# One 4.5 MB weight load made as eight interleaved loads of sixteen rows each

## The chip, the cores and the metric

The kernel runs on one core of one Trainium2 chip. The metric is the device time of one execution in microseconds (us); the lower the better. Times are medians of several runs.

## The reference

Two independent problems, A and B, have the same shapes, and their results are put side by side. Each is one decoding step of attention with a sliding window over a cache:

```python
W = min(4096, max(256, Sk // 4))                       # 4096 of 16384 cached positions
q = (x @ wq).reshape(B, 1, Hq, Dh).transpose(0,2,1,3)  # x 2x1x576, wq 576x4096
k = repeat(k_cache[:, :, Sk - W:, :], 2, axis=1)       # 2x16x16384x128 -> 32 heads
v = repeat(v_cache[:, :, Sk - W:, :], 2, axis=1)
p = softmax(einsum("bhqd,bhkd->bhqk", q, k) * Dh ** -0.5)
o = einsum("bhqk,bhkd->bhqd", p, v)
out = o.transpose(0,2,1,3).reshape(B, 1, Hq * Dh) @ wo # wo 4096x576
# result: concatenate([A, B], axis=-1)
```

All inputs are bf16. B is 2, Hq 32, Hkv 16, Dh 128. Nearly all bytes are the windows of k_cache and v_cache: 2 problems x 2 batches x 16 heads x 4096 x 128 x 2 bytes, twice, which is 134 MB. The two wq are 4.7 MB each and the two wo as much.

## The kernel before, in words

The program is written as lists of operations, one list for each engine, in an order set by hand (`_Sched`, lines 28 to 58). Each operation names the operations that it depends on; `emit` puts semaphore waits ahead of it. A transfer adds 16 to its semaphore when it has landed, so whoever needs it waits for 16 times the number of transfers (`dma_op`, which counts with `n_dmas`).

**The load queue.** All large loads are issued by SyncE (SP), in program order, onto one queue that the 16 DMA engines serve: first wq of A (`wq0`), then wq of B (`wq1`), both at line 187, then the stream of cache slabs at line 378 (K0, K1, K2, then K and V in turn, 16 of each, 4 MB a slab), with blocks of wo (line 362) between them. ScalarE's queue carries only the small loads of x (line 179) and one store.

**The ring.** A tile `ring` of four slots of 128 partitions x 32 KB takes the slabs. Before the slabs it holds the two wq, each spread over 128 partitions with 36,864 bytes (9 blocks of 2048 bf16) in each: partition p gets the p-th of 128 equal parts of wq's bytes. So wq0 and wq1 lie over the first three slots. Slab K0 goes to the fourth slot and waits for nothing. K1 goes to the first slot and waits until the matmuls of wq0 are done (`first_deps`); K2 waits for those of wq0 and wq1. From then on SP issues a slab when the last reader of its slot is done.

**From wq to q.** DVE spreads x out (`xs`, line 222) and transposes it (`xT`, line 229). TensorE then computes q of problem A from wq0 with 36 matmuls (`q0`, lines 279 and 264), and of problem B from wq1 (`q1`), waiting for `wq_dma[P]`, that is for the semaphore of that load. ScalarE takes q out of PSUM, TensorE transposes and spreads it, and GpSimd makes masked copies of it (`zq`).

**Each K slab** is transposed by DVE in two halves (line 433) and multiplied by q on TensorE (lines 459 and 264). Two slabs (one group of four heads, both batches) give the scores of one softmax: DVE takes the maximum (467), ScalarE the exponentials (497), DVE transposes them (506). **Each V slab** is multiplied by these (536), scaled and reduced on DVE (559, 566). At intervals the heads' results are multiplied by wo (618, 639), and the two outputs are stored.

The change touches the loop at lines 184 to 188, which issues `wq0` and `wq1`:

```python
for P in range(NPROB):
    def f_wq(e, P=P):
        src = probs[P][3].rearrange("a b -> (a b)").rearrange("(p f) -> p f", p=128)
        return e.dma_start(ringf[:, P * QW:(P + 1) * QW], src).then_inc(wq_sem[P], 16)
    wq_dma[P] = dma_op("sp", wq_sem[P], 1, f_wq, [], "wq%d" % P)
```

Its readers are `f_q` (the matmuls of q), which waits for `wq_dma[P]`, and, through the order of SP's queue, every later load.

Of the kernel before, what the change touches and what calls it, by code (L numbers as in the profile page):

```python
# [62 lines left out]
def build_kernel(nc, probs, out):  # L63
# [25 lines left out]
    QW = NU * UW  # L89
# [3 lines left out]
    with es:  # L93
# [50 lines left out]
        ringf = ring[:].rearrange("p r f -> p (r f)")  # L144
# [16 lines left out]
        wq_sem = [sem("wq%d" % P) for P in range(NPROB)]  # L161
# [7 lines left out]
        def dma_op(eng, sem_h, n_dmas, fn, deps, tag):  # L169
            op = S.add(eng, fn, deps, tag)  # L170
            dma_count[sem_h] = dma_count.get(sem_h, 0) + 16 * n_dmas
            op.dma = (sem_h, dma_count[sem_h])
            return op
# [9 lines left out]
        wq_dma = {}  # L183
        for P in range(NPROB):
            def f_wq(e, P=P):
                src = probs[P][3].rearrange("a b -> (a b)").rearrange("(p f) -> p f", p=128)
                return e.dma_start(ringf[:, P * QW:(P + 1) * QW], src).then_inc(wq_sem[P], 16)
            wq_dma[P] = dma_op("sp", wq_sem[P], 1, f_wq, [], "wq%d" % P)

        pool = lambda fn, deps, tag: S.add("pool", fn, deps, tag)  # L190
        dve = lambda fn, deps, tag: S.add("dve", fn, deps, tag)
# [600 lines left out]
def bass_concat_heads__sliding_block_cached__sliding_block_cached__decode_kernel(  # L792
    nc, A_x, A_k_cache, A_v_cache, A_wq, A_wo, B_x, B_k_cache, B_v_cache, B_wq, B_wo, out,
):
    build_kernel(nc, [(A_x, A_k_cache, A_v_cache, A_wq, A_wo), (B_x, B_k_cache, B_v_cache, B_wq, B_wo)], out)
# [28 lines left out]
```

## Time and profile before

| what | value | where from |
|---|---|---|
| median of 3 runs | 363.08 us (362.99 to 363.29) | times |
| span of the profiled execution, first to last instruction | 361.8 us | page |
| median of the runs less that span | 1.3 us | worked out |
| bytes moved by DMA | 153.26 MB, 424 GB/s over the span | page, part 2 |
| share of the 16 DMA engines' time used by SP's queue | 98.7% | page, part 3 |
| TensorE, VectorE, ScalarE busy | 66%, 60%, 13% of the span | page, part 1 |
| granted TensorE clock, mean | 0.849 | view of the cores |
| wq0 from issue to landing | 13.3 us | page, part 6 |
| wq1 from issue to landing | 23.8 us | page, part 6 |

The profile gives no time of the profiled execution but its span; the runs' own times include what lies around the span, and 1.3 us is the difference to their median.

How to read the views: the page's part 2 cuts the span into 40 slices and gives, for each, the share of time that the engines and the 16 DMA engines were busy (in tenths) and the GB/s moved. Part 3 adds up the packets of each DMA queue: q1 is SP's queue, q10 ScalarE's. Here one row of a transfer, that is the contiguous bytes for one partition, is one packet, and each DMA engine that took part in a transfer adds a packet of 4 bytes, which increments the semaphore. Part 6 lists the transfers by the line that issued them, with their size and the median time from issue to landing. The timeline lists instructions in order of time; SPq and ACTq are the issues of transfers on SP's and ScalarE's queues. The windows give each engine's busy time, the DMA share and the GB/s in stretches of the span.

### The profile page before, as it was taken

The page shows a single profiled execution, that of the slowest core. Times are in us where ns is not written, and L with a number is a line of the kernel's source. Part 1 is how long each engine was busy: PE and PEld are TensorE (multiplying, and loading weights), DVE is VectorE, ACT ScalarE, POOL GpSimd, SP SyncE. Part 2 cuts the span into 40 slices and gives each one's busy share as a digit, 9 for nine tenths or more (in the row PEclk, how much of TensorE's full clock was granted, in tenths as well). Part 3 has the DMA queues.
Part 4 walks back from the last instruction along what each step waited for, and adds up shares of the span by engine and source line. Part 5 has one row for each costly group of instructions (what it writes and reads, how often), then busy time and mean ns, then how long its engine had stood idle before and what let it go on. Part 6 is the DMA issues. An engine that isn't in the chain of part 4 may idle for free.

```text
span 361.8 us, 2625 instructions
## 1 busy us (share of the span) xinstructions
PE 240.2 (66%) x1292; PEld 57.2 (16%) x927; DVE 218.7 (60%) x150; ACT 46.0 (13%) x78; POOL 24.3 (7%) x84
## 2 busy tenths in 40 slices
PE   0497787666485747662596675567776875668695
PEld 0000111112111201111121121112112121112222
DVE  1901898495929591934909585682927776674622
ACT  1002100040023000500005000500005000500500
POOL 4200101100010001000010000100010001000000
PEclk9999698969988996888788796888688796868969
DMA  8999999999999999999999999999999999999996
GB/s 327 457 435 406 460 408 446 424 431 438 417 453 408 457 404 428 444 431 431 435 420 444 417 449 410 440 431 438 424 442 412 449 417 429 435 435 431 417 412 256
DMA packets 6227, 153.26 MB, mean 424 GB/s; under 512 B 700, under 2 KB 840, under 8 KB 1224
## 3 DMA queue, kind: packets, MB, share of 16 engines
q1 hardware_dynamic: 6196, 153.10, 98.7%
q8 instruction: 8, 0.13, 0.1%
q14 instruction: 3, 0.02, 0.0%
q10 hardware_dynamic: 20, 0.01, 0.0%
HBM read 153.10 MB, written 0.00 MB: 423 GB/s over the span
## 4 chain that ended last, share of the span: by engine, by line
DMA 48%; DVE 26%; PE 16%; issue 8%; ACT 1%; POOL 0%; SPq 0%
DMA ring<-in_B_k_cache_dram 17%; DVE xt L433 16%; DMA ring<-in_A_k_cache_dram 13%; DMA ring<-in_B_v_cache_dram 9%; DMA ring<-in_B_wq_dram 7%; PE st L264 5%; PE st L459 5%; DMA wob<-in_B_wo_dram 3%; PE pj L264 2%; DVE oR L566 2%; DVE mx L467 2%; DVE pT L506 2%; DVE tmp L559 2%; PE ot L536 2%; PE pj L618 1%
## 5 line engine op out<-in xcount | busy, mean ns | idle before, releaser
L459 PE MATMUL st<-xt,zq 128*128 128x512 bf16 x256 | 124.1, 485 | 86.1 <-DVE xt L433 86.1
L433 DVE STREAM_TRANSPOSE xt<-ring 128x4096 f32<-128x4096 f32 x32 | 141.5, 4427 | 28.0 <-DMA ring<-in_A_k_cache_dram 18.8
L264 PE MATMUL st<-xt,zq 128*128 128x512 bf16 x256 | 122.7, 479 | 0.0
L497 ACT ACTIVATE pR<-st,bias 128x512 bf16<-128x512 f32 x32 | 40.0, 1414 | 222.9 <-DVE bias L490 222.9
L459 PEld LDWEIGHTS st<-xt,zq 128*128 128x128 bf16 x256 | 29.4, 115 | 210.1 <-issue 107.7
L536 PE MATMUL ot<-ring,pT 128*32 128x512 bf16 x512 | 32.6, 396 | 3.9 <-DMA ring<-in_B_v_cache_dram 3.9
L490 DVE SCALAR_TENSOR_TENSOR bias<-vmask,tb,offm 128x4 f32<-128x4 f32 x8 | 1.8, 223 | 43.0 <-PE tb L487 43.0
L520 DVE TENSOR_REDUCE ssum<-tb 128x2 f32<-128x8 f32 x8 | 1.3, 162 | 36.0 <-PE tb L517 36.0
L425 POOL TENSOR_TENSOR zq<-qs,bmask 128x64 bf16<-128x64 bf16 x32 | 8.7, 293 | 168.1 <-PE st L264 145.8
L506 DVE STREAM_TRANSPOSE pT<-pR 128x2048 bf16<-128x2048 bf16 x8 | 18.4, 2303 | 0.8 <-ACT pR L497 0.7
L279 PE MATMUL ot<-ring,pT 128*32 128x512 bf16 x18 | 7.6, 421 | 15.0 <-DMA ring<-in_A_wq_dram 14.2
L559 DVE SCALAR_TENSOR_TENSOR tmp<-ot,rsb,dmask 128x512 f32<-128x512 f32 x16 | 11.5, 719 | 7.9 <-PE ot L536 7.9
L566 DVE TENSOR_REDUCE oR<-tmp 128x128 f32<-128x512 f32 x15 | 15.6, 1042 | 0.5
L536 PEld LDWEIGHTS ot<-ring,pT 128*32 128x32 bf16 x512 | 12.4, 99 | 19.6 <-DMA ring<-in_B_v_cache_dram 5.5
L618 PE MATMUL pj<-wob,oM 128*2 128x288 bf16 x48 | 12.7, 299 | 0.0
L264 PE MATMUL pj<-wob,oM 128*2 128x288 bf16 x48 | 12.7, 299 | 0.0
L264 PE MATMUL pj<-ring,pT 128*32 128x512 bf16 x36 | 11.9, 416 | 0.0
L467 DVE TENSOR_REDUCE mx<-st 128x2 f32<-128x1024 f32 x8 | 9.7, 1213 | 0.1
L497 ACT ACTIVATION_READ_ACCUMULATOR pR<-st,bias 128x1 f32 x32 | 8.8, 276 | 0.0
L264 PE MATMUL st<-ring,pT 128*32 128x512 bf16 x18 | 7.3, 407 | 0.0
L222 DVE TENSOR_TENSOR xt<-xt,hmask 4x1152 bf16<-4x1152 bf16 x2 | 2.7, 1349 | 6.7 <-DMA xt<-in_A_x_dram 6.7
L469 POOL TENSOR_TENSOR mv<-mx,v 128x2 f32<-128x2 f32 x8 | 1.6, 195 | 75.8 <-DVE mx L467 75.8
(68 smaller groups left out, 75.6 us busy)
## 6 DMA issues: line engine op xcount, KB each, us to landing
ring<-in_A_k_cache_dram SPq DMA_DIRECT2D x8, 4096.0 KB, 24.3
ring<-in_A_v_cache_dram SPq DMA_DIRECT2D x8, 4096.0 KB, 29.9
ring<-in_B_k_cache_dram SPq DMA_DIRECT2D x8, 4096.0 KB, 27.0
ring<-in_B_v_cache_dram SPq DMA_DIRECT2D x7, 4096.0 KB, 29.8
ring<-in_A_wq_dram SPq DMA_DIRECT2D x1, 4608.0 KB, 13.3
ring<-in_B_wq_dram SPq DMA_DIRECT2D x1, 4608.0 KB, 23.8
wob<-in_A_wo_dram SPq DMA_DIRECT2D x2, 2304.0 KB, 28.3
wob<-in_B_wo_dram SPq DMA_DIRECT2D x1, 2304.0 KB, 27.4
```

The source lines that it names most:

```text
L264: return e.add_instruction(mybir.InstMatmult(name=nc.get_next_instruction_name(), engine=mybir.EngineType.PE, ins=[e.lower_ap(mv_), e.lowe ...
L279: last = e.matmul(QB[c], wt, mv_, start=first, stop=True, skip_group_check=True)
L425: last = e.tensor_tensor(dst, src, msk, ALU.mult)
L433: Xop[(t, jh)] = dve(lambda e: e.transpose(xt[:, jh, :].bitcast(FP32).rearrange("p (kp x kt) -> p x kp kt", kp=2, kt=2), ring[:, r, jh * H ...
L459: last = e.matmul(ob, wt, mv_, start=first, stop=True, skip_group_check=True)
L467: ch[(G, "max")] = dve(lambda e: e.tensor_reduce(mx[:], st[:, :].rearrange("p (x t) -> p t x", t=2), AX.X, ALU.max), [Sop[(2 * G + 1, 1)]] ...
L497: last = e.activation(pR[:].rearrange("p (x k) -> p k x", k=4)[:, kv, :], st[:, :].rearrange("p (x t) -> p t x", t=2)[:, kv % 2, :], ACTF.Exp,
L506: pT_op[G] = dve(lambda e: e.transpose(pT[:, v, :].rearrange("p (w j q) -> p j w q", w=4, q=8), pR[:].rearrange("p (j w q) -> p j w q", w= ...
L536: last = e.matmul(OTB[32 * c:32 * c + 32, :], pT[:, v, base + 32 * c:base + 32 * c + 32], ring[:, r, jj * 128:(jj + 4) * 128], start=rd == ...
L559: evac_op[i] = dve(lambda e: e.scalar_tensor_tensor(tv, o, rsb[:, v, b:b + 1], dm, ALU.mult, ALU.mult), deps, "ev%d" % i)
L566: ch[(G, "red%d" % b)] = dve(lambda e: e.tensor_reduce(oR[:, b, :], tmp[:].rearrange("p (j d) -> p d j", j=4), AX.X, ALU.add), [evac_op[i] ...
L618: last = e.matmul(PJ[h], oM[:, j, :], mv_, start=start and j == 0, stop=True, skip_group_check=True)
```

## The change

The load of wq0 becomes eight transfers, all on SP's queue, all ahead of wq1. The transfer number s takes the rows (partitions) s, s+8, s+16, up to s+120: sixteen rows of 36,864 bytes, from the same addresses as before to the same places. Each adds 16 to the same semaphore, and `dma_op` is told of eight transfers, so that `q0` waits for 128. The load of wq1 and all else stay.

```diff
             def f_wq(e, P=P):
                 src = probs[P][3].rearrange("a b -> (a b)").rearrange("(p f) -> p f", p=128)
-                return e.dma_start(ringf[:, P * QW:(P + 1) * QW], src).then_inc(wq_sem[P], 16)
-            wq_dma[P] = dma_op("sp", wq_sem[P], 1, f_wq, [], "wq%d" % P)
+                dst = ringf[:, P * QW:(P + 1) * QW]
+                if P > 0:
+                    return e.dma_start(dst, src).then_inc(wq_sem[P], 16)
+                for s in range(8):
+                    last = e.dma_start(dst[s:128:8, :], src[s:128:8, :]).then_inc(wq_sem[P], 16)
+                return last
+            wq_dma[P] = dma_op("sp", wq_sem[P], 1 if P else 8, f_wq, [], "wq%d" % P)
```

## The prediction

> **What bounds the kernel.** I read the page's parts on DMA first. Part 2 (busy share of the 16 DMA engines and GB/s, in 40 slices of 9 us), part 3 (queues) and part 6 (issues):
>
> ```profile
> DMA  8999999999999999999999999999999999999996
> GB/s 327 457 435 406 460 408 446 424 431 438 417 453 408 457 404 428 444 431 431 435 420 444 417 449 410 440 431 438 424 442 412 449 417 429 435 435 431 417 412 256
> DMA packets 6227, 153.26 MB, mean 424 GB/s; under 512 B 700, under 2 KB 840, under 8 KB 1224
> ...
> q1 hardware_dynamic: 6196, 153.10, 98.7%
> ...
> q10 hardware_dynamic: 20, 0.01, 0.0%
> ...
> ring<-in_A_wq_dram SPq DMA_DIRECT2D x1, 4608.0 KB, 13.3
> ring<-in_B_wq_dram SPq DMA_DIRECT2D x1, 4608.0 KB, 23.8
> ```
>
> Only the first and the last slice are below 9. SP's queue fills 98.7% of the engines' 361.8 us, 357.1 us, so only 4.7 us are not used. The windows show where:
>
> ```profile
> 0.00:1.80 1.80, 0.00 (x0) 0.00 (x0) 0.14 (x1) 0.00 (x0) 1.06 (x8) 1.00 0.00 1
> 1.80:14.20 12.40, 0.00 (x1) 0.01 (x1) 5.83 (x12) 1.28 (x1) 4.32 (x12) 1.00 1.04 429
> 14.20:25.10 10.90, 10.11 (x37) 1.00 (x10) 3.78 (x5) 0.00 (x0) 1.42 (x2) 1.00 0.99 427
> 25.10:100.00 74.90, 52.05 (x229) 10.70 (x129) 50.95 (x20) 8.44 (x18) 4.72 (x18) 0.89 1.01 434
> ...
> 357.00:361.80 4.80, 2.30 (x32) 1.04 (x28) 0.77 (x2) 0.40 (x1) 0.00 (x0) 1.00 0.29 112
> ```
>
> The last two columns are the DMA share and the GB/s. 1.8 us pass before the first byte, some 3 us at the end; between them the engines never run dry together. The chain of waits puts 26% on DVE and 16% on PE, but that is the chain of slot releases: SP is told early enough, the next slab is queued by the time the engines reach it. So a delay of the load stream goes to the end in full: there is no idle time in which it could be made good.
>
> The limit is not shared by all. The packet records give 1.364 us for nearly every row of 36,864 bytes and 1.216 us for one of 32,768: 27.0 GB/s for one engine in both. In the last window, where engines finish one by one, the packets of 1152 bytes take 51 ns while many engines run and while four do. So each engine runs at a limit of its own, or of its own way into the memory that it writes. That distinction decides this case.
>
> **The start**, from the timeline:
>
> ```profile
> 0.80 0.81 ACTq L179 DMA_DIRECT2D xt<-in_A_x_dram  x2
> ...
> 0.80 0.39 SPq L187 DMA_DIRECT2D ring<-in_A_wq_dram  x1
> ...
> 1.25 0.41 SPq L187 DMA_DIRECT2D ring<-in_B_wq_dram  x1
> ...
> 14.20 0.61 PE L279 MATMUL ot<-ring,pT 128*32 128x512 bf16 x1 [14.20 <-DMA ring<-in_A_wq_dram]
> ```
>
> wq0 is issued at 0.80, lands at 14.1 (issue + 13.3), and q0 begins. The packet records: 15 engines start their first row between 1.82 and 2.19, one at 2.88; the first rows end by 4.27, then each engine takes a row every 1.36 us. 128 rows on 16 engines are 8 rows each, 10.9 us.
>
> **The change part by part.**
>
> 1. *Seven more issues on SP.* An issue takes 0.39 to 0.41 us, and the timeline's next begins 0.45 after; x's transfers of two rows take 0.40 each, so it is not the rows that cost. wq1 is issued at 0.80 + 8 x 0.45 = 4.4 instead of 1.25, K0 at 4.9 instead of 1.71. On the path: nothing. An engine needs 1.36 us for its row and gets one every 0.45; wq1 is needed when wq0's rows end, about 13 us, 8 us later. Without that cover it would cost 3.2 us. SP has no wait before K1; ScalarE's queue with x isn't moved.
>
> 2. *Seven more completions.* 43 transfers on SP's queue with 16 completions each are 688 of the small packets. One takes 9 ns; seven on each engine cost 0.06 us, on the path.
>
> 3. *An earlier start.* The first piece has 16 rows to hand out, not 128. Bounds: no gain (the issue of two rows takes as long as that of 128), and at most the ramp's excess: from the first packet to the last end of a first row are 2.45 us for a row of 1.36, so 1.09 us. I take half of the 0.38 us over which 15 first packets start, 0.19 us, as the row nearest to handing out.
>
> 4. *Which rows are in flight together.* Before, the engines move 429 GB/s through 128 rows at once. After, the first four pieces hold only partitions whose number leaves 0 to 3 when divided by eight, sixteen at a time, then 4 to 7. If an engine had eight neighbouring rows before, it has the same rows in the same order now and this costs nothing. But no record names the partition that an engine writes. What the trace has: x's four transfers of two rows and the two stores leave 20 packets on q10 and 4 on q1, a row and a completion on each of two engines; so neighbouring partitions go to different engines there, rows are dealt by position in the transfer, and a piece of 16 rows gives each engine one. That does not tell how 128 are dealt. Bounds: nothing from below (27.0 GB/s is the most that any packet has, so no gain), and from above rows that share a way: two sharing make 8 x 1.364 = 10.9 us more, four sharing three times that, 32.7 us. Between ends so far apart I take two sharing, +10.9 us. Every long packet of this trace, whatever its size, runs at the same rate whether 16 or fewer engines are busy. A fixed rate for each way does that, and a mix of rows that was never seen can keep such a rate or lose it; the least that it can lose, when partners go in step, is half.
>
> [...]
>
> 5. *What follows.* q0 starts about 10.7 us later, at 24.9; it ends 10 us after that, before wq1 lands (now 24.28 and 25.07). K1 waits for q0, which stays one slab ahead of need. x has landed by then, even if its packets wait behind longer rows. All later stages move by the same amount.
>
> **Sum.** Against the profiled execution: 361.8 + 10.91 + 0.06 - 0.19 = 372.6 us of span; with the 1.3 us by which the median lies above the span, 373.9 us.
>
> **The rivals.**
>
> - *Nothing happens* (the engines had neighbouring rows, or nothing is shared): 363.08 + 0.06 - 0.19 = 362.9 us. For it: the ways may be the engines' own, and nothing in the trace shows two of them meeting. Against it: it needs the new mix of rows to be as good as the only one seen. This decides if rows of wq0 keep 1.364 us.
> - *Faster*: the same, and the small first piece removes the whole excess of the ramp, 1.09 us: 362.0 us. It decides if the 16 first rows end by 3.2 instead of 4.27. Against it: a row's first packet takes 1.8 us or more on 15 engines, after it has begun, which looks like a latency that pieces don't take away.
> - *Sharing part of the time*: one partner gets ahead by up to four rows and they no longer meet; between a quarter and three quarters of the 10.9 us, 365.8 to 371.3, middle 368.5. For it: starts are up to 1.05 us apart.
> - *Four on one way*: 363.08 + 32.7 = 395.8 us.
>
> **How the numbers follow.** Two sharing in step 0.70 (own range 371.8, ramp excess of 1.09 gone and a lead of 1.05 used, to 375.1, the slowest first row, 2.35 us, doubling as well, 0.98 more, and 0.2 for the highest run); part of the time 0.10; four 0.02; nothing 0.13; faster 0.05. The range from 365.8 to 375.1 holds the first two, 0.80. Beyond 0.2% (0.7 us, about what a measurement can tell from no change): slower 0.82, same 0.13, faster 0.05.
>
> **What would show it.** Right: rows of wq0 take about 2.7 us in the packet records, those of wq1 1.36 again; wq0 takes 24 us from issue to landing; the first two slices move half of the others' GB/s; q1 has 6308 packets (7 x 16 more); L187 has nine issues 0.45 us apart; the windows after wq0 look like those of before, 10.7 us later. Wrong: wq0 lands at 14 again (then nothing is shared), or it lands late and later windows run faster than 434 GB/s, or SP's issues come slower than a row each 1.36 us.

## The result and the profile after

The changed kernel takes 375.39 us (median of 4 runs, 375.10 to 375.49) against 363.17 us: 1.0333 times the time of before, interval 1.032 to 1.0345. The direction of the forecast held, and rows of wq0 take 2.86 us instead of 1.364, near the twofold time that it assumed; the size of the total did not hold: 373.9 us were forecast, and the range ended at 375.1, 0.3 us below the measured median.

The page after (parts 2, 3 and 6; a slice is now 9.35 us):

```profile
DMA  9999999999999999999999999999999999999996
GB/s 190 189 252 434 448 441 399 447 438 420 431 441 433 413 446 432 427 426 427 441 431 419 438 431 434 431 422 438 424 438 430 431 431 431 429 431 434 413 416 255
DMA packets 6339, 153.26 MB, mean 410 GB/s; under 512 B 812, under 2 KB 952, under 8 KB 1336
...
q1 hardware_dynamic: 6308, 153.10, 98.6%
...
ring<-in_A_wq_dram SPq DMA_DIRECT2D x8, 576.0 KB, 13.9
ring<-in_B_wq_dram SPq DMA_DIRECT2D x1, 4608.0 KB, 31.5
```

The two lines that matter are the first two. The DMA engines are as busy as before, 98.6%, and yet the first two slices move less than half of the later ones, 190 and 189 GB/s. The busy share says that packets were under way, not how fast they went. From the fourth slice on the rates are those of before. The 6308 packets are the 112 more that seven transfers with sixteen completions each make.

The windows of the kernel after, cut at the stages:

```profile
4.00:24.00 20.00, 0.00 (x0) 0.00 (x0) 9.62 (x16) 0.00 (x0) 3.54 (x8) 1.00 1.01 207
27.00:36.00 9.00, 9.00 (x31) 0.83 (x7) 0.00 (x0) 0.00 (x0) 0.00 (x0) 1.00 0.98 422
36.00:112.00 76.00, 55.81 (x234) 11.00 (x129) 51.05 (x20) 8.44 (x18) 4.72 (x18) 0.87 1.01 433
```

While wq0 loads, the share is 1.01 and the rate 207 GB/s; while wq1 loads, whole as before, 422. Before, the same stretch from 4 to 24 us moved 428 GB/s:

```profile
4.00:24.00 20.00, 9.80 (x36) 0.98 (x9) 9.61 (x16) 0.00 (x0) 3.54 (x8) 1.00 0.99 428
```

A packet's bytes count where it starts, so windows with the same time per row can differ by some per cent (428 here, 443 in two runs further down, with rows of 1.364 us in all three). The chain of events is in the timeline:

```profile
0.80 5.08 SPq L191 DMA_DIRECT2D ring<-in_A_wq_dram  x8
...
5.93 0.59 SPq L189 DMA_DIRECT2D ring<-in_B_wq_dram  x1
...
6.51 1.35 DVE L227 TENSOR_TENSOR xt<-xt,hmask 4x1152 bf16<-4x1152 bf16 x1 [4.96 <-DMA xt<-in_A_x_dram]
...
26.72 0.10 PEld L284 LDWEIGHTS ot<-ring,pT 128*32 128x32 bf16 x1 [26.72 <-DMA ring<-in_A_wq_dram]
```

SP needs 0.64 us for each of the eight issues, not 0.45, and the matmuls of q wait for wq0 until 26.72 us instead of 14.20.

The packet records show where the time went. Sixteen packets at a time in order of their starts, which should be one for each engine (no record names the engine); means in us:

| step | before | after | difference |
|---|---|---|---|
| start of the first row | 2.03 | 2.46 | +0.43 |
| first row of wq0 | 1.97 | 2.65 | +0.69 |
| the other seven rows of wq0 | 9.55 (1.364 each) | 20.02 (2.86 each) | +10.47 |
| first row of wq1 | 1.37 | 1.88 | +0.51 |
| the other seven rows of wq1 | 9.52 | 9.55 | +0.03 |
| sum | | | +12.13 |

The spans differ by 374.1 - 361.8 = 12.3 us, so 12.13 of it has happened by the end of wq1, and all later stages carry it unchanged.

### The profile page after: what moved, and what is told of

Its sections match the earlier page's. It is cut to its first block, busy times and chain, and to the rows that moved or that the text cites. A ratio compares the mean times of both kernels' runs of the same rounds, so it can differ in the third digit from the quotient of the medians.

```text
span 374.1 us, 2633 instructions
## 1 busy us (share of the span) xinstructions
PE 236.6 (63%) x1293; PEld 56.9 (15%) x927; DVE 218.8 (58%) x150; ACT 45.9 (12%) x78; POOL 24.3 (6%) x84
## 3 DMA queue, kind: packets, MB, share of 16 engines
q1 hardware_dynamic: 6308, 153.10, 98.6%
## 4 chain that ended last, share of the span: by engine, by line
DMA 56%; DVE 20%; PE 13%; issue 7%; SPq 1%; ACT 1%; POOL 0%
DMA ring<-in_B_k_cache_dram 24%; DMA ring<-in_A_k_cache_dram 12%; DVE xt L438 12%; DMA ring<-in_B_v_cache_dram 9%; DMA ring<-in_B_wq_dram 8%; PE st L269 4%; PE st L464 4%; DMA wob<-in_B_wo_dram 3%; DVE oR L571 2%; DVE mx L472 2%; PE pj L269 2%; PE ot L541 1%; ACT pR L502 1%; DVE tmp L564 1%; SPq L191 1%
## 5 line engine op out<-in xcount | busy, mean ns | idle before, releaser
L464 PE MATMUL st<-xt,zq 128*128 128x512 bf16 x256 | 121.5, 474 | 87.7 <-DVE xt L438 87.7
L269 PE MATMUL st<-xt,zq 128*128 128x512 bf16 x256 | 120.0, 469 | 0.0
L541 PE MATMUL ot<-ring,pT 128*32 128x512 bf16 x512 | 34.1, 410 | 7.6 <-DMA ring<-in_B_v_cache_dram 7.6
L284 PE MATMUL ot<-ring,pT 128*32 128x512 bf16 x18 | 7.8, 434 | 26.8 <-DMA ring<-in_A_wq_dram 26.7
L564 DVE SCALAR_TENSOR_TENSOR tmp<-ot,rsb,dmask 128x512 f32<-128x512 f32 x16 | 11.5, 718 | 12.8 <-PE ot L541 12.8
L541 PEld LDWEIGHTS ot<-ring,pT 128*32 128x32 bf16 x512 | 12.8, 101 | 24.1 <-DMA ring<-in_B_v_cache_dram 10.2
L269 PE MATMUL pj<-ring,pT 128*32 128x512 bf16 x36 | 12.2, 423 | 0.0
L623 PE MATMUL pj<-wob,oM 128*2 128x288 bf16 x48 | 12.1, 289 | 0.0
L269 PE MATMUL pj<-wob,oM 128*2 128x288 bf16 x48 | 12.0, 287 | 0.0
L284 PEld LDWEIGHTS ot<-ring,pT 128*32 128x32 bf16 x18 | 1.9, 105 | 42.4 <-DMA ring<-in_A_wq_dram 26.7
```

The costliest lines, as they stand in the source:

```text
L269: return e.add_instruction(mybir.InstMatmult(name=nc.get_next_instruction_name(), engine=mybir.EngineType.PE, ins=[e.lower_ap(mv_), e.lowe ...
L284: last = e.matmul(QB[c], wt, mv_, start=first, stop=True, skip_group_check=True)
L464: last = e.matmul(ob, wt, mv_, start=first, stop=True, skip_group_check=True)
L541: last = e.matmul(OTB[32 * c:32 * c + 32, :], pT[:, v, base + 32 * c:base + 32 * c + 32], ring[:, r, jj * 128:(jj + 4) * 128], start=rd == ...
L564: evac_op[i] = dve(lambda e: e.scalar_tensor_tensor(tv, o, rsb[:, v, b:b + 1], dm, ALU.mult, ALU.mult), deps, "ev%d" % i)
L623: last = e.matmul(PJ[h], oM[:, j, :], mv_, start=start and j == 0, stop=True, skip_group_check=True)
```

## The experiments

The theory: which partitions a transfer writes sets the time of its rows. The prediction put this as ways into the memory that engines share; that is a supposition, since no record names a way. Rival 1: it is the eight transfers as such (issues, completions, start). Rival 2: it is the source, whose rows are read at a distance of 294,912 bytes. All diffs are against the changed kernel, and "row" is a packet of 36,864 bytes.

**Eight transfers by columns.** All 128 rows in each.

```diff
-                    last = e.dma_start(dst[s:128:8, :], src[s:128:8, :]).then_inc(wq_sem[P], 16)
+                    last = e.dma_start(dst[:, s * 2304:(s + 1) * 2304], src[:, s * 2304:(s + 1) * 2304]).then_inc(wq_sem[P], 16)
```

> wq0 in eight transfers as in the change, but cut by columns: each transfer has all 128 rows and 4608 bytes of each. Theory (a row's way into the memory is shared by the two engines that write it at the same time; cutting as such costs little): packets of 4608 bytes take 0.178 us as the last wo blocks' do, 64 of them on each engine are 11.4 us against 10.9, and 0.06 us for completions: 363.5 to 364.0 us. Rival 1 (eight transfers on the queue cost the time: slower issues of 0.59 us, later start, more completions): 370 us or more. Rival 2 (rows that lie 294,912 bytes apart in the source are read slowly together): no such rows here, 363.5 to 364.0 us as well.

Measured: 363.73 us, 1.0011 times before (1.0002 to 1.002). The page's part 2 and the line of wq0:

```profile
GB/s 297 449 420 456 405 457 409 452 416 441 427 434 429 428 438 415 426 448 419 448 419 436 430 427 419 451 419 441 423 441 419 441 427 423 429 448 416 423 417 251
...
ring<-in_A_wq_dram SPq DMA_DIRECT2D x8, 576.0 KB, 7.3
```

No slice is at half of its rate. Eight issues, eight sets of completions and smaller packets cost half a microsecond together (the kernel before took 363.23 us beside this run). Rival 1 falls: it is not the number of transfers. The first packet starts at 1.82 us as before, so cutting gives no earlier start either.

**Sixteen neighbours.**

```diff
-                    last = e.dma_start(dst[s:128:8, :], src[s:128:8, :]).then_inc(wq_sem[P], 16)
+                    last = e.dma_start(dst[16 * s:16 * s + 16, :], src[16 * s:16 * s + 16, :]).then_inc(wq_sem[P], 16)
```

> wq0 in eight transfers of sixteen rows, but neighbouring rows, 16s to 16s+15. [...] Rival 1 (eight transfers as such): as the change, 375.4 us. Rival 2 (distance of rows in the source): the sixteen rows of a transfer are one block of the source, so near the kernel before, 363 to 364 us.

Measured: 392.11 us, 1.0796 (1.0779 to 1.0812). Part 2 of its page:

```profile
DMA  9999899999999999999999999999999999999996
GB/s 121 121 121 121 302 450 429 429 428 429 429 429 429 429 428 430 430 444 433 429 429 429 428 433 429 430 437 436 433 429 431 427 429 429 418 439 433 421 417 268
```

More than four slices at 121 GB/s, again with busy engines. The same bytes in as many transfers of as many rows as in the change, but neighbouring partitions: a little over a quarter of the full rate, not half. Rows take 5.02 us, 3.7 times 1.364. Rivals 1 and 2 both said something else.

**The partitions of the change, another source.**

```diff
-                    last = e.dma_start(dst[s:128:8, :], src[s:128:8, :]).then_inc(wq_sem[P], 16)
+                    last = e.dma_start(dst[s:128:8, :], src[16 * s:16 * s + 16, :]).then_inc(wq_sem[P], 16)
```

> As the change for the partitions written (s, s+8, ...), but the sixteen rows of a transfer come from one block of the source, rows 16s to 16s+15. The rows of wq0 thus go to the wrong partitions, so q of problem A is computed from permuted weights; sizes and order of work stay. Theory: only the partitions written count, 375.2 to 375.6 us and rows of 2.9 us. Rival 1 (eight transfers as such): the same. Rival 2 (distance of rows in the source): 363 to 364 us and rows of 1.36 us.

Measured: 374.45 us, 1.0305 (1.0291 to 1.032), 0.9 us less than the change. The window of 4 to 24 us:

```profile
4.00:24.00 20.00, 0.00 (x0) 0.00 (x0) 9.62 (x16) 0.00 (x0) 3.54 (x8) 1.00 1.01 214
```

214 GB/s instead of 207; most rows take 2.83 us instead of 2.86 to 2.90. The time is below the bounds that I gave, so the source may have a share, but of at most 0.9 us in 12. Even that is not shown: wq0 in the run with both wq split, further down, has the partitions and the source of the change, and most of its rows take 2.83 to 2.85 us. Rival 2 falls as the main cause.

**Sixteen neighbours, distant sources.** The counterpart of the last.

```diff
-                    last = e.dma_start(dst[s:128:8, :], src[s:128:8, :]).then_inc(wq_sem[P], 16)
+                    last = e.dma_start(dst[16 * s:16 * s + 16, :], src[s:128:8, :]).then_inc(wq_sem[P], 16)
```

> Sixteen neighbouring partitions for each of the eight transfers of wq0, as in the run with neighbours, but read from rows s, s+8, ... of the source, so that 294,912 bytes lie between the rows read together. Rows of wq0 go to the wrong partitions: q of problem A is computed from permuted weights. Theory (the partitions written set the time): rows of 5.0 us again, 391.5 to 392.7 us. Rival (the source sets part of it, as 2.83 against 2.88 us in the earlier pair of runs hints): rows of 5.1 us or more, 393 us or more. The first transfer of the strided patterns starts 0.4 us later; if the step of the partitions written does that, this run starts at 1.82 us, if that of the source does, at 2.2.

Measured: 391.91 us, 1.0789 (1.0758 to 1.0821), rows of 4.99 us: the same as with neighbouring sources. The window of 6 to 40 us:

```profile
6.00:40.00 34.00, 0.00 (x0) 0.00 (x0) 9.60 (x16) 0.00 (x0) 1.15 (x5) 1.00 1.01 118
```

Of four runs with two patterns of partitions and two of sources, the time follows the partitions. The first packet starts at 1.82 us and the eight issues take 3.76 us, where the change has 2.21 and 5.08, and the run before, with strided partitions alone, 2.21 and 5.65. So the later start comes from the step between the partitions written, not from the source and not from the number of rows.

**Four transfers of 32 rows.**

```diff
-                for s in range(8):
-                    last = e.dma_start(dst[s:128:8, :], src[s:128:8, :]).then_inc(wq_sem[P], 16)
+                for s in range(4):
+                    last = e.dma_start(dst[s:128:4, :], src[s:128:4, :]).then_inc(wq_sem[P], 16)
                 return last
-            wq_dma[P] = dma_op("sp", wq_sem[P], 1 if P else 8, f_wq, [], "wq%d" % P)
+            wq_dma[P] = dma_op("sp", wq_sem[P], 1 if P else 4, f_wq, [], "wq%d" % P)
```

> [...] Rival 1 (number of transfers): half of the change's loss, some 369 us.

**Two transfers of 64 rows.** The same with `range(2)`, a step of 2 and a count of 2.

> [...]

Measured: 363.48 us in both, 1.0005 (0.9996 to 1.0014) and 1.0005 (0.9995 to 1.0015). The windows of 4 to 24 us, first with 32 rows, then with 64:

```profile
4.00:24.00 20.00, 9.36 (x34) 0.98 (x9) 9.62 (x16) 0.00 (x0) 3.54 (x8) 1.00 1.03 443
```

```profile
4.00:24.00 20.00, 9.28 (x33) 1.00 (x9) 9.63 (x16) 0.00 (x0) 3.56 (x8) 1.00 1.03 443
```

Full rate, rows of 1.364 us. The 369 us that rival 1 gives for 32 rows were not measured. With 32 rows at a step of four partitions, and with 64 at a step of two, nothing is lost but the later start, which is there too (first packets at 2.18 and 2.14 us). So a step between the partitions does not by itself cost the rate: sixteen rows at a step of eight move 207 GB/s, 32 at a step of four 443. How rows are dealt to the engines is not shown. Every run with transfers of sixteen rows lost rate; whether another pattern of sixteen can keep it was not tested.

**Both wq split.**

```diff
-                if P > 0:
-                    return e.dma_start(dst, src).then_inc(wq_sem[P], 16)
                 for s in range(8):
                     last = e.dma_start(dst[s:128:8, :], src[s:128:8, :]).then_inc(wq_sem[P], 16)
                 return last
-            wq_dma[P] = dma_op("sp", wq_sem[P], 1 if P else 8, f_wq, [], "wq%d" % P)
+            wq_dma[P] = dma_op("sp", wq_sem[P], 8, f_wq, [], "wq%d" % P)
```

> The change on both loads: wq0 and wq1 each in eight transfers of rows s, s+8, .... Theory (what is lost is lost row by row): eight more rows of 2.88 us instead of 1.364 are 12.1 us, of which the 0.5 us that wq1's first row already loses in the change are no news: 386.5 to 387.5 us. Rival (the loss belongs to the beginning, when the queue and the memory start, and the later start of 0.4 us is part of it): 375.4 to 377 us.

Measured: 386.90 us, 1.0651 (1.0634 to 1.0668). Part 2 of its page:

```profile
GB/s 185 233 195 203 219 432 435 435 423 432 415 432 432 430 429 434 435 427 432 432 432 425 434 435 432 421 438 435 429 429 434 433 432 435 427 429 429 430 406 254
```

Five slices at half rate instead of somewhat over two. The second load costs 11.5 us more, though SP issues it between 5.93 and 10.94 us, while wq0 still loads. So the loss is one of the rows, not of the beginning, and it about doubles with the number of such rows (23.7 us against 12.2).

**Every fourth partition of one half** and **every second of a quarter.** Sixteen rows still, spread over 64 partitions in the first run and over 32 in the second, where those of the change are spread over all 128.

```diff
-                    last = e.dma_start(dst[s:128:8, :], src[s:128:8, :]).then_inc(wq_sem[P], 16)
+                    r = slice(64 * (s // 4) + s % 4, 64 * (s // 4) + 64, 4)    # first run
+                    r = slice(32 * (s // 2) + s % 2, 32 * (s // 2) + 32, 2)    # second run
+                    last = e.dma_start(dst[r, :], src[r, :]).then_inc(wq_sem[P], 16)
```

> wq0 in eight transfers of sixteen rows, every fourth partition of one half (0 to 63 in the first four, 64 to 127 in the last four). [...] Rival (the loss comes from the step of eight partitions, or from rows 294,912 bytes apart in the source): rows of 1.364 us or some other time, 363.3 to 364 us if nothing else is lost.

> [...]

Measured: 375.12 us, 1.0327 (1.0308 to 1.0345), and 375.22 us, 1.033 (1.03 to 1.036). The windows of 4 to 24 us of the first and the second:

```profile
4.00:24.00 20.00, 0.00 (x0) 0.00 (x0) 9.62 (x16) 0.00 (x0) 3.55 (x8) 1.00 1.00 207
```

```profile
4.00:24.00 20.00, 0.00 (x0) 0.00 (x0) 9.62 (x16) 0.00 (x0) 3.56 (x8) 1.00 1.01 207
```

The same 207 GB/s as the change, with steps of 4 and 2 instead of 8, and rows of 2.87 us in the second run. So the loss does not come from the step of eight, nor from rows 294,912 bytes apart. Sixteen strided rows lose about half of the rate at all three steps, sixteen neighbours more (118 GB/s), and 32 rows at a step of four or 64 at a step of two lose nothing (443). What in these sets of partitions makes the difference is not shown.

The packet records hold one more detail, again sixteen rows at a time. The fifth rows of the change, with which its last four transfers begin, take 2.71 us, the others after the first 2.86 to 2.90. The run with both wq split passes three times from one set of four transfers to the next, and each time the rows are short (2.64 to 2.65 us, the others after the first 2.83 to 2.86). The second run here goes to its next block of 32 partitions with the third, the fifth and the seventh rows; only the fifth are short (2.73 us, the others 2.87). What shortens these rows is not shown.

**Two queues.** The last four transfers on ScalarE's queue, behind x's, with a semaphore of their own, for which the matmuls of q wait too.

```diff
-                for s in range(8):
+                for s in range(4):
                     last = e.dma_start(dst[s:128:8, :], src[s:128:8, :]).then_inc(wq_sem[P], 16)
...
+        def f_wqb(e):
+            src = probs[0][3].rearrange("a b -> (a b)").rearrange("(p f) -> p f", p=128)
+            for s in range(4, 8):
+                last = e.dma_start(ringf[s:128:8, 0:QW], src[s:128:8, :]).then_inc(wqb_sem, 16)
+            return last
+        wqb_dma = dma_op("act", wqb_sem, 4, f_wqb, [], "wqb")
...
-            q_done[P] = pe(f_q, [wq_dma[P], d_xT[P]], "q%d" % P)
+            q_done[P] = pe(f_q, [wq_dma[P], wqb_dma, d_xT[P]], "q%d" % P)
```

> The change with its last four transfers (s from 4 to 7) issued by ScalarE's queue behind x's, beside the first four on SP's; the matmuls of problem A wait for both. [...] Rival (the number of transfers or of issues): 375 to 376 us.

Measured: 375.98 us (374.67 to 378.24), 1.0356 (1.0313 to 1.0399). The profiled execution is the slowest of the four. Its windows:

```profile
4.00:24.00 20.00, 0.00 (x0) 0.00 (x0) 9.63 (x16) 1.28 (x1) 3.55 (x8) 1.00 1.02 234
24.00:36.00 12.00, 2.42 (x6) 0.25 (x2) 0.00 (x0) 0.00 (x0) 0.00 (x0) 1.00 0.96 310
```

234 GB/s is an eighth more than the 207 of one queue, and wq0 lands later, at 33.6 us, since rows of wq1 come between its own. The second queue does not bring back the full rate. Up to 10 us nearly all rows are SP's, of 2.86 us after each engine's first; from 10 to 17 us rows of both queues are under way, and most take 2.64 to 2.67 us. The time is that of the change (375.39 us). The rival gives it as well, but for another reason: eight transfers by columns took 363.73 us, so neither the number of transfers nor that of issues makes this time.

## Why the prediction was wrong, point by point

Two terms of the sum failed. Step 3 put the start at a gain of 0.19 us, and it was a loss of 0.43 us. Step 4 put the shared rows at 10.91 us, each at exactly twice 1.364, and wq1's first row at nothing; the slower rows cost 11.67 us together.

*What bounds the kernel* held. The load stream has no idle time, and 12.13 us lost by the end of wq1 are 12.3 us at the end.

*Step 1, the issues*, had the wrong size (0.64 us apart, not 0.45) and the right place: they are hidden, since a row takes 2.86 us. The trace before gave no firm price: x's issues of two rows are not 0.40 us each but 0.24 to 0.53, and the whole load of K0 took 0.61.

*Step 2, the completions*: they take 18 ns instead of 9 while wq0 loads; 0.1 us, and it is contained in the 2.86 us of a row.

*Step 3, the start*, failed in its sign. I expected 0.19 us of gain from fewer rows to hand out. The first rows start 0.43 us later, because the partitions are strided; with columns or neighbours the first packet stays at 1.82 us. That is 0.62 us of the miss.

*Step 4, the shared rows*, had the right direction and too small a size. That two rows share, and not one or four, did not follow from the trace: it was my estimate, a choice between 0 and 32.7 us. No run shows two engines on one way, so none shows this term; what the runs show in its place is that the time goes with the partitions written (sixteen rows at steps of 8, 4 and 2 move 207 GB/s, sixteen neighbours 118). I set a shared row at twice 1.364, 2.73 us. It takes 2.86, and wq1's first row is slow as well, 0.51 us (the first of the sixteen to start takes 2.02 us, while rows of wq0 are still under way, the last 1.42); why is not shown. The three rows of the table that belong to it, 0.69 + 10.47 + 0.51 = 11.67 us, stand against 10.91 + 0.06 forecast: 0.70 us of the miss. Start and shared rows are 1.3 of the 1.5 us by which 375.39 lies over 373.9; the rest, 0.2 us, lies in the small change between the end of wq1 and the end of the span.

*Step 5* held: wq1's matmuls begin at 37.51 us, right after wq0's last (37.07 and 0.38 us long), and from 36 us on the windows are those of before. x came earlier, not later (DVE starts on it at 6.51, not 8.25 us).

*The range* allowed the slowest first row to double and nothing for a later start. Its lower end, 371.8, takes 0.19 us twice: from 373.9 it would be 372.0. A sign that was open had been given the bounds "no gain" and "all of it"; a loss belonged there.

*The rivals*: "nothing happens", "faster" and "part of the time" were all wrong. "Four on one way", 395.8 us, is near what sixteen neighbours took (392.11 us), but four strict shares would make rows of 5.46 us, where 5.02 were measured, and no run shows a way.

## What to carry to other kernels

Its bytes and its number of rows did not tell the rate of this load: which partitions lie in one transfer decided it, and patterns of sixteen rows moved 207 or 118 GB/s where whole transfers move 430. Whoever cuts a load should cut along the row (columns cost 0.1%) or keep 32 rows spread over all partitions (no cost clear of noise here), and read the GB/s of the stage beside the busy share, since DMA engines that the page shows as busy ran at little over a quarter of their rate here (118 of 430 GB/s). And an effect whose sign the trace leaves open needs a bound on both sides.

## What was not expected of the hardware

- A transfer to every second, fourth or eighth partition took 0.57 to 0.61 us to issue (medians of the runs) and began at 2.14 to 2.23 us; one to neighbouring partitions 0.39 to 0.47 us, beginning at 1.82. The whole load of wq1 is issued slowly behind strided ones (0.59 us; behind sixteen neighbours 0.42), but K0's takes 0.57 to 0.73 us in every run, so what makes a whole load's issue slow is not shown. A strided source did not do this (0.47 us an issue and a first packet at 1.82 us, with neighbouring partitions written). The later start moves the first rows by 0.3 to 0.5 us; the total time of the runs with 32 and 64 rows cannot tell that from nothing.
- Sixteen strided rows take 2.86 us each in the change and sixteen neighbours 5.02, that is 2.1 and 3.7 times 1.364. Why these are not whole shares is open; the step (207 GB/s at 8, 4 and 2) and the source (2.83 and 4.99 us with the other one) don't explain it.
- Transfers of 32 rows at step 4 or of 64 at step 2 kept the full rate (rows of 1.364 us, 443 GB/s); sixteen at step 8, or at steps 4 and 2 within a half or a quarter of the partitions, did not (207 GB/s).
